# Mask rows by a POOL transfer, chunk bounds in another PSUM bank, and a planner that counts DMA transposes as late

## The chip, the cores and the metric

The kernel runs on one core of one Trainium2 chip. The metric is the device time of one execution in microseconds (us); the median of 8 runs is given with the lowest and the highest. The engines are TensorE (PE; PEld is its weight load), VectorE (DVE), ScalarE (ACT), GpSimd (POOL) and SyncE (SP). PE writes to PSUM, which has eight banks; the other working memory is SBUF. POOL and SP issue the DMA transfers here.

## What is computed

Attention in which each query sees only a few chunks of keys, followed by a feed-forward layer (FFN) with a squared relu:

```python
B, H, S, D = 4, 8, 768, 64          # chunk = 32, nc = 24, top_k = 6
k_min, k_max = min and max of k over each chunk
ub = sum over d of maximum(q * k_min, q * k_max)          # bound of each query and chunk
ub = where(causal by chunk, ub, -1e9)
top_chunks = argsort(ub)[..., -top_k:]
scores = (q @ k.T) / sqrt(D)
scores = where(chunk in top_chunks and pos_q >= pos_k, scores, -1e9)
attn = softmax(scores);  a = attn @ v
x = a as [3072 tokens, 512]
out = maximum(x @ w_in, 0) ** 2 @ w_out                   # w_in 512 x 2048, w_out 2048 x 512
```

The first 128 queries of each batch have at most four chunks before them, so all of these are chosen, and no selection is made for them.

## The kernel before

**Tiling.** There are 4 batches `b`, and in each 4 head pairs `hp`, which makes 16 pairs `p = 4 b + hp`. A sequence is six tiles of 128 tokens. The first tile of every batch is handled apart (`first_attention`, and one FFN over the four first tiles); the other five tiles of a batch (NS = 5) go through two stages for each pair and then through that batch's FFN.

**Stage A of a pair** (`stage_a`) prepares the operands of its scores. Keys and queries are needed with the head dimension on the partitions. For batches 0 and 1 PE transposes them (`kT`, `qT`, in PSUM); for batches 2 and 3 (`b >= BY_DMA`) SP issues DMA transposes (L377) from loaded tiles `nt` into `kt` and `qt`. From these VectorE takes the maximum and the minimum of each chunk (`kr`, L681), and the positive and the negative part of the queries (`qp`, `qm`, L697). Ten small products on PE give the bounds `ub` (L647, L649). VectorE adds the chunk mask (`ubm`, L706), takes the eight largest (`m8`, L655) and compares (`selb`, L711). The selection is transposed to `sT` (by PE, or for batches 2 and 3 by a DMA transpose) and copied under the queries, into rows 64 to 87 of `qsc`. Rows 64 to 87 of the keys' operand `kqc` hold the mask's rows: -32768 where the chunk of that row is. So one product of 88 rows (L766) gives scores with the mask added.

**The mask's rows** (`kq_rows`, L326 to L337) are the same for all pairs. `kqc` has four sets of two heads, eight slots, which the pairs use in turn. The first slot is written by ScalarE (L328), the second is copied by a transfer that SP issues (L333), and the other six by one more transfer of SP (L335). Scores of pair 0 need the first two, those of every other pair the third step (the list `prepared` in `stage_a`).

**Stage B** (`stage_b`) runs, for each head, five score banks of 512 columns (L766), the exp on ScalarE (L788), a causal mask on the diagonal tiles by VectorE (L743) or POOL (L746), and the products with the values (L777). The sums are normalised by VectorE (L594, L596) into `x`.

**The FFN** (`ffn`) transposes `x` to `xT`, forms the hidden products `ph` (L850), takes the relu on ScalarE (L857) or VectorE (L859), squares on VectorE (`h`, L868), and adds up `py` (L881) in four parts for each 128 tokens. `py` is copied out (L271 or L273) and stored by SP (L894).

**PSUM banks.** Each buffer has a tag, and a tag a number of banks: `tp` 1, `ps` 3, `av` 2, `ff` 2. Scores, the bounds `ub` and PE's `sT` all have the tag `ps`; `kT` and `qT` have `tp`; `ph`, `py` and PE's `xt` have `ff` (in the last batch `ph` has `ps`). A buffer is given a bank when the last reader of an earlier buffer of its tag is done.

**What sets the order.** Nothing is scheduled by hand. Every operation is recorded with a cost on each engine that may run it, a due time, the operations that it needs and its buffers (`Plan.op`). `Plan.order` then plays the program: it looks for the operation that can start first, takes among those of that engine within a small wait the one that is due first, and books its cost. `Transfers` plays the two DMA queues, one for POOL's loads and one for what SP issues, which share a rate. The sequence found is written out, and each engine runs its part in that order. The due times hang on the parameters `P`: `lead` says how many steps of the plan ahead of its turn each pair's stage A is due, `f_due` the same for the first tiles, `rate` and `due` spread the FFNs, `va`, `vm`, `ra` and `h2` shift single kinds, and `loads` and `later` are the order of POOL's loads. Only POOL's loads have a fixed order; each also waits until no more than eight are on their way. In `loads`, a small letter with a number is that head pair of batch 0 (two transfers), a capital is the first tile of that batch, and `i` and `o` are quarters of the two weight matrices.

Of the kernel before, what the change touches and what calls it, by code (L numbers as in the profile page):

```python
# [9 lines left out]
F32 = mybir.dt.float32  # L10
# [31 lines left out]
class Transfers:  # L42
# [10 lines left out]
    def run(self, queues, until):  # L53
        now = self.now
        while now < until and any(queues.values()):
            active = [q for q in queues.values() if q]
            rate = self.RATE / len(active)
            span = min([until - now] + [q[0][1] / rate for q in active])
            now += span
            for q in active:  # L60
                q[0][1] -= span * rate
                if q[0][1] < 1e-6:
                    op = q.pop(0)[0]
                    op.end = now + (0.85 if op.turns else 0.35)
        return until if until < 1e8 else now
# [12 lines left out]
class Plan:  # L78
# [19 lines left out]

    def op(self, where, due, fn, needs=(), tiles=(), packets=0, turns=False):
        op = Op(where, due, fn, [n for n in needs if n is not None],  # L100
                [t for t in tiles if t is not None], packets, turns)
        for t in op.tiles:
            t.users.append(op)
        op.number = -1 if packets and not turns else len(self.ops) - len(self.loads)
        self.ops.append(op)
        if packets and not turns:
            self.loads.append(op)
        return op
# [92 lines left out]
def kernel(  # L201
# [9 lines left out]
    nc = tc.nc  # L211
# [19 lines left out]
    NSET = 4  # L231
    P = dict(lead=[38, 70, 77, 66, 65, 20, 16, 23, 34, 24, 32, 68, 19, 63, 66, 67],
             f_due=[-89, -30, -320.97, -400.97], sp='K0 Q0 K1 Q1', rows=-379,
             rows_after=0, up_due=-1.28, up_rate=3.88, half=4, due=[-6, 1, 3, 45],
             rate=[3.07, 2.84, 4.48, 1.87], va=13.9, vm=5.92, ra=2.68, h2=-1.11,
             later='k1 q1 v1 q2 k2 q3 v3 v2 k3', shift={}, p0=-5650, wait=0.01,
             loads="k0 Q3 K3 q0 Q2 K2 V0 V3 V2 V1 v1 "
                   "k1 i0 v0 i3 q1 i2 v2 k2 i1 q2 o0 q3 k3 o1 o2 v3 o3")

# [86 lines left out]
    def kq_rows(i):  # L326
# [5 lines left out]
        elif i == 1:  # L332
            nc.sync.dma_start(out=kqs[D:KC, 0, 1], in_=kqs[D:KC, 0, 0])  # L333
        else:
            nc.sync.dma_start(  # L335
                out=kqs[D:KC, 1:].rearrange("c s hh j -> c (s hh) j"),
                in_=kqs[D:KC, 0, 0:1].to_broadcast([NC, 2 * NSET - 2, S]))  # L337
# [11 lines left out]
    def load(key, fn, due, packets, tiles=(), cost=0.88):  # L349
        op = plan.op({"POOL": cost}, due, fn, tiles=tiles, packets=packets)  # L350
        loaded.setdefault(key, []).append(op)
# [23 lines left out]

    def turn_by_dma(dst, src, due, needs, tiles, packets=1270):
        return plan.op({"SP": 1.2}, due, lambda _: nc.sync.dma_start_transpose(  # L377
            out=dst(), in_=src()), needs, tiles, packets=packets, turns=True)

# [35 lines left out]
    def load_turned(nm, b, j, due):  # L415
# [3 lines left out]
        else:  # L419
# [9 lines left out]
            lambda: (src.tile if src else firsts[nm][:, b]).rearrange(  # L429
                "p h d -> p (h d)"), due, needs, [src, dst])  # L430
        loaded.setdefault((nm, b), []).append(op)
# [46 lines left out]
    for what in P["loads"].split():  # L478
        i = int(what[1])
        if what[0] == "i":  # L480
            load_w_in(4 * i, 4 * i + 4, -980)
        elif what[0] == "o":
            load_w_out(4 * i, 4 * i + 4, -980)
        elif what[0].isupper():
            load_first(what[0].lower(), i, -980)
        else:
            load_pair(what[0], 0, i, -980)
# [113 lines left out]
    def rows(after):  # L601
        made["rows", 0] = plan.op({"ACT": 0.84}, P["rows"], lambda _: kq_rows(0),
                                  [made["ident"]] + after)
        for i in (1, 2):
            made["rows", i] = plan.op({"SP": 0.5}, P["rows"] + i, lambda _, i=i: kq_rows(i),
                                      [made["rows", 0]], packets=(200, 1200)[i - 1],
                                      turns=True)

# [4 lines left out]
    def stage_a(p):  # L613
# [10 lines left out]
        qp, qm = buffer("qp", [128, QC]), buffer("qm", [128, QC])  # L624
        ub = buffer("ps", [128, NS, 2, NC], F32, name="ub")
        ubm = buffer("ubm", [128, NS, 2, NC], F32)
# [42 lines left out]
        if b >= BY_DMA:  # L669
            got = list(loaded["k", b])  # L670
            kc_on, qc_on, q_on = {"DVE": 0.36}, {"DVE": 0.40}, 0.39
        else:
# [42 lines left out]
        if b >= BY_DMA:  # L715
            t = turn_by_dma(lambda: sT.tile, lambda: selbs[:, s].rearrange(
                "p t h c -> p (t h c)"), t0 + 21, [sel], [sT], 950)
        else:
# [88 lines left out]
    def ffn(x, ready, rows, by_dma, due, rate, up_tags=("ff", "ff")):  # L807
# [12 lines left out]
        def turn(t):  # L820
            if by_dma:
                xt_made.append(turn_by_dma(
                    lambda: xT[:, t], lambda: x[:, t], step(0.225), ready(t),
                    [xT] + xs))
                return
# [14 lines left out]
        def up(f, c0, c1, i):  # L840
            tag = up_tags[i % 2]
            w = c1 - c0
# [78 lines left out]
    for b in range(B):  # L921
        x = buffer("x", [128, NS, d_model])
        x_done[b, 1] = []
        for p in range(NP * b, NP * (b + 1)):
# [4 lines left out]
            x, lambda t, b=b: x_done[b, 1], [S * b + 128 * t for t in range(1, NT)],  # L929
            0 < b < B - 1, HALVES * NP * (b + 1) + P["due"][b], P["rate"][b], ("ps", "ps") if last else ("ff", "ff"))  # L930
        for c in range(2):
# [45 lines left out]
```

## Time and profile before

| | |
|---|---|
| median of 8 runs | 265.15 us (264.58 to 266.77) |
| the profiled execution | 264.91 us, of which the span from the first to the last instruction is 263.2 us |
| mean granted clock of PE | 0.992 |
| DMA | 26.11 MB in 103808 packets, the queue of POOL's loads 66.9% of 16 engines' span |

The costliest groups, as the page gives them (line, engine, operation, tiles and shapes, count, then busy us and mean ns of one, then the idle time before them and what ended it):

```profile
L788 ACT ACTIVATE e<-ps 128x512 bf16<-128x512 f32 x160 | 89.0, 607 | 12.4 <-PE av L777 6.7
L850 PE MATMUL ph<-xT,w_in_sb 128*128 128x256 bf16 (+2 forms) x592 | 97.1, 304 | 0.4
L881 PE MATMUL py<-w_out_sb,h 128*128 128x512 bf16 (+2 forms) x400 | 92.5, 370 | 0.0
L868 DVE TENSOR_TENSOR h<-ht 128x256 bf16<-128x256 bf16 (+2 forms) x148 | 47.1, 326 | 14.4 <-ACT ht L857 10.3
L766 PE MATMUL ps<-qsc,kqc 88*128 88x128 bf16 (+1 forms) x320 | 54.7, 272 | 2.2 <-DVE ubm L706 1.5
```

A matmul's mean is longer than the time from one to the next, since they are pipelined: four products of 512 columns follow each other in 0.86 us. The span falls into a start of some 24 us, in which few tiles have landed, a long middle in which attention and FFN are interleaved, and from 206 us on only the last FFN.

### The profile page before, as it was taken

How to read it: one execution, taken by the hardware profiler on the slowest of the kernel's cores; microseconds unless marked ns; L12 is line 12 of the kernel's file. 1: busy time of each engine (PE TensorE's matmuls, PEld its weight loads, DVE VectorE, ACT ScalarE, POOL GpSimd, SP SyncE). 2: the span in 40 equal slices, each digit the busy share in tenths (PEclk: the TensorE clock that was granted, in tenths of full speed). 3: DMA queues.
4: the chain of work that ended last, by engine and by line, in shares of the span. 5: the costliest groups of instructions: out<-in, count | busy, mean ns of one | idle time of the engine just before them, and what ended most of it. 6: DMA issues, size and time to landing. Idle time of an engine off the chain costs nothing.

```text
span 263.2 us, 6518 instructions
## 1 busy us (share of the span) xinstructions
PE 252.4 (96%) x2391; PEld 162.2 (62%) x2391; DVE 195.2 (74%) x687; ACT 181.4 (69%) x372; POOL 104.9 (40%) x182
## 2 busy tenths in 40 slices
PE   7679999999999999998999999999999999999995
PEld 3447656665787665565686665567876548565443
DVE  5699899979998999999999979856777403455000
ACT  1679687974599978795888867688998315276112
POOL 8998778698347698632221221120012000000000
PEclk9799999999999999999999999999999999999999
DMA  9999999999999999964540001345000021100222
GB/s 143 167 174 186 188 181 197 157 116 196 188 99 135 143 155 155 159 115 112 114 104 4 0 2 55 87 110 115 2 0 2 0 80 42 41 4 0 80 80 80
DMA packets 103808, 26.11 MB, mean 99 GB/s; under 512 B 96312, under 2 KB 100832, under 8 KB 103776
## 3 DMA queue, kind: packets, MB, share of 16 engines
q0 software_dynamic: 75088, 13.11, 66.9%
q1 hardware_dynamic: 28688, 12.59, 21.0%
q8 instruction: 18, 0.29, 0.5%
q14 instruction: 14, 0.11, 0.1%
HBM read 27.26 MB, written 6.29 MB: 127 GB/s over the span
## 4 chain that ended last, share of the span: by engine, by line
PE 62%; DVE 17%; DMA 8%; ACT 4%; SPq 3%; issue 3%; POOL 2%; POOLq 0%; DVEq 0%; ACTq 0%
PE py L881 24%; PE ph L850 22%; PE ps L766 7%; DVE kr L681 5%; PE av L777 5%; SPq L377 3%; DMA k<-in_k_dram 2%; DMA kt<-nt 2%; DVE qsc L273 2%; DVE m L655 2%; DMA qt<-nt 2%; DVE kqc L273 2%; DMA nt<-in_q_dram 2%; ACT e L788 2%; ACT ht L857 1%
## 5 line engine op out<-in xcount | busy, mean ns | idle before, releaser
L788 ACT ACTIVATE e<-ps 128x512 bf16<-128x512 f32 x160 | 89.0, 607 | 12.4 <-PE av L777 6.7
L850 PE MATMUL ph<-xT,w_in_sb 128*128 128x256 bf16 (+2 forms) x592 | 97.1, 304 | 0.4
L881 PE MATMUL py<-w_out_sb,h 128*128 128x512 bf16 (+2 forms) x400 | 92.5, 370 | 0.0
L850 PEld LDWEIGHTS <-w_in_sb 128*128 128x128 bf16 x592 | 55.7, 97 | 23.3 <-issue 1.4
L746 POOL TENSOR_SCALAR_AFFINE_SELECT e<-e 128x128 bf16<-128x128 bf16 (+1 forms) x88 | 30.2, 345 | 93.4 <-ACT e L788 90.1
L857 ACT ACTIVATE ht<-ph 128x256 bf16<-128x256 f32 (+2 forms) x121 | 54.4, 453 | 17.6 <-PE ph L850 14.0
L868 DVE TENSOR_TENSOR h<-ht 128x256 bf16<-128x256 bf16 (+2 forms) x148 | 47.1, 326 | 14.4 <-ACT ht L857 10.3
L766 PE MATMUL ps<-qsc,kqc 88*128 88x128 bf16 (+1 forms) x320 | 54.7, 272 | 2.2 <-DVE ubm L706 1.5
L881 PEld LDWEIGHTS <-h 128*128 128x128 bf16 x400 | 35.6, 98 | 31.3
L777 PEld LDWEIGHTS <-e 128*128 128x128 bf16 x640 | 35.1, 97 | 11.8 <-DVE e L743 0.3
L271 ACT COPY ob<-py 128x512 f32<-128x512 f32 (+2 forms) x23 | 13.0, 567 | 35.0 <-PE py L881 34.9
L777 PE MATMUL av<-vn,e 128*128 128x65 bf16 x480 | 35.6, 193 | 0.0
L766 PEld LDWEIGHTS <-kqc 88*128 88x128 bf16 x320 | 26.0, 97 | 12.9 <-issue 3.7
L271 ACT COPY qsc<-sT 24x384 bf16<-24x384 bf16 (+1 forms) x39 | 17.1, 437 | 4.5 <-PE sT L276 2.5
L596 DVE TENSOR_TENSOR x<-av,rc 128x320 bf16<-128x320 f32 (+1 forms) x40 | 18.9, 471 | 0.5
L655 DVE MAX8 m<-ubm 128x8 f32<-128x24 f32 x160 | 15.5, 168 | 0.2
L681 DVE TENSOR_REDUCE kr<-kT 128x24 bf16<-128x768 bf16 x16 | 14.8, 949 | 0.4 <-PE kT L276 0.3
L681 DVE TENSOR_REDUCE kr<-kt 128x24 bf16<-128x768 bf16 x16 | 15.0, 939 | 0.0
L743 DVE TENSOR_TENSOR e<-e,tri 128x128 bf16<-128x128 bf16 (+1 forms) x40 | 9.7, 247 | 6.7 <-ACT e L788 5.9
L777 PE MATMUL av<-v,e 128*128 128x65 bf16 x160 | 14.6, 193 | 0.0
L859 DVE TENSOR_SCALAR ht<-ph 128x256 bf16<-128x256 f32 (+2 forms) x27 | 12.9, 482 | 2.2 <-PE ph L850 1.9
L273 DVE COPY xT<-xt 128x512 bf16<-128x512 bf16 x10 | 4.1, 420 | 12.3 <-PE xt L276 12.3
(85 smaller groups left out, 247.3 us busy)
## 6 DMA issues: line engine op xcount, KB each, us to landing
out_dram<-ob SPq DMA_DIRECT2D x23, 256.0 KB, 2.4
w_in_sb<-in_moe_w_in_dram POOLq DMA_DIRECT2D x4, 512.0 KB, 7.9
w_out_sb<-in_moe_w_out_dram POOLq DMA_DIRECT2D x4, 512.0 KB, 8.2
vn<-in_v_dram POOLq DMA_DIRECT2D x15, 128.0 KB, 6.3
nt<-in_q_dram POOLq DMA_DIRECT2D x10, 128.0 KB, 5.0
nt<-in_k_dram POOLq DMA_DIRECT2D x10, 128.0 KB, 5.1
kn<-in_k_dram POOLq DMA_DIRECT2D x8, 80.0 KB, 6.3
qn<-in_q_dram POOLq DMA_DIRECT2D x8, 80.0 KB, 7.6
```

The lines of the kernel that those rows point to most:

```text
L271: nc.scalar.copy(dst, src)
L596: return plan.op({"DVE": 0.06 + 0.00108 * D * n}, due, lambda _: nc.vector.tensor_mul(x(), av[:, :, 0:D], rc[:, 0:n].unsqueeze(2).to_broad ...
L655: nc.vector.max(out=m8[:, i, hh], in_=ubm[:, i, hh])
L681: nc.vector.tensor_reduce(kr[:, mm].rearrange("d (t c) -> d t c", c=128 // CH) if b >= BY_DMA else kr[:, mm], part(kT).rearrange("d t (c j ...
L746: nc.gpsimd.affine_select(out=e, in_=e, compare_op=ALU.is_ge, fill=0.0, base=0, channel_multiplier=-1, pattern=[[0, n], [1, 128]])
L766: nc.tensor.matmul(ps[:, 128 * c:128 * (c + nt)], lhsT=kqs[:, s, hh, 128 * j:128 * (j + 1)], rhs=qss[:, s, hh, 128 * (t0 - 1):128 * (t0 - ...
L777: nc.tensor.matmul(av[:, t - 1], lhsT=e[:, 128 * c:128 * (c + 1)], rhs=value_tile(b, h, j), start=(i == 0 and c == 0), stop=(i == len(BANK ...
L788: nc.scalar.activation(e.tile, ps.tile, ACT.Exp, scale=scale), [sc], [ps, e])
L850: nc.tensor.matmul(ph.tile, lhsT=w_in_sb[:, ki, 128 * f:128 * (f + 1)], rhs=xT[:, c0 // 128:c1 // 128, ki], start=(ki == 0), stop=(ki == N ...
L857: nc.scalar.activation(ht.tile, ph.tile, ACT.Relu)
L868: {"DVE": 0.067 + w / 1920}, at[0] + P["h2"], lambda _: nc.vector.tensor_mul(h2[f][:, c0:c1], ht.tile, ht.tile), [op], [ht, h2[f]])))
L881: nc.tensor.matmul(py.tile, lhsT=h2[f][:, 128 * t:128 * (t + 1)], rhs=w_out_sb[:, f, c0:c1], start=(f == 0), stop=(f == NFI - 1))
```

## The change

Four things are changed in the program, and all parameters of the plan with them.

1. The third step of the mask's rows (six slots of `kqc`) is issued by POOL instead of SP, as one of its loads: it stands as `R2` in `loads`, behind the third head pair of keys. It still waits for the first slot.
2. The bounds `ub` of pairs 8 to 15 have the tag `tp` instead of `ps`.
3. The plan adds a time `late` to the end of DMA transfers: 0.5 for loads, 4.5 for the transposes of keys and queries, 3.5 for those of selections, 3.0 for those of `x`. It is a number in the planner alone.
4. The costs that the plan books on VectorE for copies of DMA-transposed tiles go from 0.36, 0.40 and 0.39 to 0.45, 0.45 and 0.42, and the transfer of the second slot is booked with 400 packets instead of 200.

```diff
-                    op.end = now + (0.85 if op.turns else 0.35)
+                    op.end = now + (0.85 if op.turns else 0.35) + op.late
...
-    P = dict(lead=[38, 70, 77, 66, 65, 20, 16, 23, 34, 24, 32, 68, 19, 63, 66, 67],
-             f_due=[-89, -30, -320.97, -400.97], sp='K0 Q0 K1 Q1', rows=-379,
-             rows_after=0, up_due=-1.28, up_rate=3.88, half=4, due=[-6, 1, 3, 45],
-             rate=[3.07, 2.84, 4.48, 1.87], va=13.9, vm=5.92, ra=2.68, h2=-1.11,
-             later='k1 q1 v1 q2 k2 q3 v3 v2 k3', shift={}, p0=-5650, wait=0.01,
-             loads="k0 Q3 K3 q0 Q2 K2 V0 V3 V2 V1 v1 "
-                   "k1 i0 v0 i3 q1 i2 v2 k2 i1 q2 o0 q3 k3 o1 o2 v3 o3")
+    P = dict(lead=[26, 15, 48, 47, 26, 61, 5, 53, 70, 14, 26, 79, 70, 28, 8, 54],
+             f_due=[207, -206, -290.97, -438.97], sp='K0 Q0 K1 Q1', rows=-1719,
+             rows_after=0, up_due=-34.03, up_rate=11.93, half=4,
+             due=[-21, -128, -27, -2], rate=[4.44, 7.05, 5.27, 4.28], va=11.75,
+             vm=13.01, ra=0.57, h2=-0.91, later='k1 q1 v1 k2 q2 q3 v2 k3 v3', shift={},
+             p0=-7210, wait=0.01,
+             loads="k0 q0 V2 Q3 V1 K3 K2 V0 Q2 k1 V3 "
+                   "i0 q1 v0 i3 i2 v1 k2 R2 q2 i1 o0 q3 k3 o1 v2 v3 o2 o3")
...
-            nc.sync.dma_start(
+            nc.gpsimd.dma_start(
                 out=kqs[D:KC, 1:].rearrange("c s hh j -> c (s hh) j"),
                 in_=kqs[D:KC, 0, 0:1].to_broadcast([NC, 2 * NSET - 2, S]))
...
+        elif what[0] == "R":
+            load("rows", lambda _: kq_rows(2), -980, 2300)
+            made["rows", 2] = loaded["rows"][0]
...
-        for i in (1, 2):
-            made["rows", i] = plan.op({"SP": 0.5}, P["rows"] + i, lambda _, i=i: kq_rows(i),
-                                      [made["rows", 0]], packets=(200, 1200)[i - 1],
-                                      turns=True)
+        made["rows", 1] = plan.op({"SP": 0.5}, P["rows"] + 1, lambda _: kq_rows(1),
+                                  [made["rows", 0]], packets=400, turns=True)
+        made["rows", 2].needs.append(made["rows", 0])
...
-        ub = buffer("ps", [128, NS, 2, NC], F32, name="ub")
+        ub = buffer("tp" if b >= BY_DMA else "ps", [128, NS, 2, NC], F32, name="ub")
...
-            kc_on, qc_on, q_on = {"DVE": 0.36}, {"DVE": 0.40}, 0.39
+            kc_on, qc_on, q_on = {"DVE": 0.45}, {"DVE": 0.45}, 0.42
```

The remaining lines of the diff pass `late` to the transposes and replace `i % 2` by `i % len(up_tags)`, which is the same here. In both programs the same products, reductions and copies are made, but for some more products with the constant tile `warm`, which the planner puts where it expects PE to idle at the start.

## The prediction

> **What bounds the kernel now.** I read the page from the top, then the busy time by stretches, the list of waits of each engine, and last the timeline around the longest waits of TensorE.
>
> ```profile
> span 263.2 us, 6518 instructions
> PE 252.4 (96%) x2391; PEld 162.2 (62%) x2391; DVE 195.2 (74%) x687; ACT 181.4 (69%) x372; POOL 104.9 (40%) x182
> ```
>
> TensorE is busy for 252.4 of 263.2 us, so 10.8 us is all that better cover could win. The stretches say where these lie (the columns are the stretch, its length, then PE, PEld, DVE, ACT and POOL busy):
>
> ```profile
> 0.00:24.00 24.00, 18.48 (x176) 10.50 (x177) 17.82 (x71) 14.70 (x28) 22.80 (x34) 0.93 1.73 166
> 24.00:55.00 31.00, 30.64 (x329) 19.91 (x327) 29.75 (x109) 24.87 (x49) 23.52 (x37) 1.00 1.69 177
> 55.00:75.00 20.00, 19.93 (x200) 13.45 (x199) 17.46 (x57) 12.71 (x27) 12.39 (x17) 1.00 1.73 163
> 75.00:100.00 25.00, 24.88 (x271) 17.93 (x270) 23.95 (x85) 22.64 (x49) 19.21 (x29) 1.00 1.91 137
> 100.00:130.00 30.00, 28.49 (x311) 17.37 (x310) 29.50 (x103) 23.40 (x46) 13.01 (x29) 1.00 1.22 132
> 130.00:160.00 30.00, 29.72 (x280) 20.55 (x278) 28.09 (x101) 24.68 (x55) 6.92 (x19) 1.00 0.13 30
> 160.00:206.00 46.00, 46.00 (x499) 31.52 (x497) 33.85 (x126) 38.05 (x79) 7.05 (x21) 1.00 0.20 53
> ```
>
> Of the 10.8 us, 5.5 lie before 24 us (24.00 less 18.48), about 2.9 are the last copy and its store, and only 2.3 lie between 24 and 206 us. Of those, 1.5 are in one stretch, 100 to 130 us, where VectorE is busy for 29.50 of 30.00: there TensorE waits, and the engine it waits for has no room. The waits name it:
>
> ```profile
> PE ps L766 <- DVE ubm L706: 1.5, 3, 0.7
> ...
> POOL nt L421 <- issue: 1.1, 4, 0.5
> ```
>
> Scores (L766) wait three times for the add that masks the chunk bounds (L706). No operand passes between these two: `ub` and the scores' `ps` share one tag with three PSUM banks, and a bank is free only when the add has read it. The timeline at the first of them:
>
> ```profile
> 103.25 0.60 PE L766 MATMUL ps<-qsc,kqc 88*128 88x128 bf16 x4
> 103.68 0.53 PE L777 MATMUL av<-vn,e 128*128 128x65 bf16 x12
> 104.05 0.22 PE L777 MATMUL av<-v,e 128*128 128x65 bf16 x2
> 104.11 0.23 PE L777 MATMUL av<-vn,e 128*128 128x65 bf16 x2
> 104.88 0.60 PE L766 MATMUL ps<-qsc,kqc 88*128 88x128 bf16 x4 [0.55 <-DVE ubm L706]
> ```
>
> The bounds were written at 103.0 to 103.2; the add ran only at 104.42, behind two reductions of 0.94 each.
>
> **The change, part by part.** The diff turns nearly every knob of the planner, so the order of all engines is new; I compared the two orders of instructions (they hold no time) and priced what differs by rows of this trace. Where I count TensorE work between two instructions, 512 columns cost 0.216 us (the chain has four such products in 0.86), a value product 0.03, a bounds product 0.027.
>
> *Bounds of pairs 8 to 15 into the transposes' bank.* `tp` has one bank, used by the transposes of pairs 0 to 7 alone and so empty afterwards. All three named waits, at 104.88, 120.47 and 129.48, come from such bounds (0.55 + 0.66 + 0.28 = 1.5). In the new order the users of `tp` from pair 8 on stand at least 3.9 us of TensorE work apart, and scores are never behind these adds. Start to start the first wait is nearer 0.7 (104.88 less the last value product at 104.14), so at most about -2.0; if VectorE's lag only shows up at the next consumer, 0. I take **-1.5**. What hides the late add now: the selection made from it goes into scores some ten microseconds of TensorE work later (pairs 8 to 12).
>
> *Scores' banks.* Without these bounds the reuse loosens: counted in the orders, scores that start less than 1.0 us of TensorE work after the previous scores of their bank go from six to three. The exp that empties a bank takes 0.607 in the mean row, and with hand-overs at both ends a gap of 0.64 to 0.89 is short by about 0.2 each: 3 x 0.2, **-0.6**, bounds -1.0 and 0.
>
> *Rows for seven mask copies by a POOL transfer.* It leaves SP at 11.13 us (0.85 of SP, which then waits till 57.60, so nothing there gains) and stands behind the third pair of key loads. While it ran, loads that had landed 0.8 to 1.3 apart came 2.4 apart (15.33, 17.70), later catching up: about 1.1 us of transfer time leaves the start. Behind the reordered loads, the first slice of the input weights should land near 20.7 instead of 22.82 (two value loads of 0.5 each and these 1.1 fewer ahead of it). But the first hidden product at 23.84 has other things ahead of it as well, so 0 (bounds -1.1 and +0.6). The new place: POOL pays one issue more, by its load rows 0.9 us, with free time of 2 us between 26 and 31 us; queued behind it are loads of pairs needed after 40 us. It should land at about 31.5, and its first reader, the scores of pair 1, stands some 23 us of TensorE work in, about 36 us on the clock: 4.5 us of cover. If that cover is gone, pair 1 waits microsecond for microsecond.
>
> Here a rule speaks against the change. The rows: POOL's loads took 0.855 to 1.1 us each while VectorE was busy for 29.75 of 31.00 (24 to 55 us), so descriptors were never held up by more than a fifth of a microsecond. The Trainium skill ("SBUF — State Buffer", section "A bandwidth-pool intuition that's wrong (but worth ruling out)") says that a transfer issued by GpSimd can be starved while VectorE holds the port that they share, 620 ns becoming 3100. By that rule the copy would come up to 2.5 us later, still inside its cover; by the row, not at all.
>
> *The start.* Query tiles of pair 0 load third instead of fifth, so VectorE's wait of 0.73 before `qp` at 13.58 goes, and ScalarE takes two query copies (0.69 against 0.49). But the preset and value products of batch 1 stand ahead of the bounds on TensorE, and batch 1's exps come after those copies. Walked by rows, bounds are at 14.45 (14.56 before), the selection ends 0.2 earlier, ScalarE's first exp of pair 0 is at 22.1 instead of 20.36, and the first hidden product at about 22.9, against 23.84, with 0.9 us less TensorE work ahead of it, so level. By the ninth hidden block I get half a microsecond late. Value **+0.3**, bounds -0.7 and +1.2.
>
> *Late transposes and truer copy costs.* These alter only the plan. SP's transposes take 1.2 each and land 1.2 to 4.6 after issue; POOL's next loads wait for their buffers (the 1.1 above, off the path). They come later now, behind more selects, and q2's last lands near 93 us with its reader at about 104. 0, bounds -0.5 and +0.5.
>
> *Where the new order is tighter.* In the FFN of batch 0 the first output tile is opened while the last hidden blocks still run, holding one of the two `ff` banks: eight hidden blocks of 384 columns then share the other, with 0.7 to 1.5 us of TensorE work between them. Emptying takes 0.495 on ScalarE plus about 0.3 of hand-over when ScalarE is free. Two of eight short by 0.1: **+0.2**, bounds 0 and +3.2. Pair 13's selection transposes now stand on SP behind four of x (1.25 each), and land about 1 us ahead of need: **+0.1**, bounds 0 and +1.0.
>
> *Sum:* -1.5 - 0.6 + 0.3 + 0.2 + 0.1 = -1.5. The profiled run took 264.91 with its span of 263.2 (1.7 around it), so it becomes 263.4; the median of the eight runs shown is 0.24 above it: **263.7**.
>
> **The rivals.** *One bank for eight hidden blocks* (slower). Place: L850 between the first and last part of batch 0's first output tile, some 84 to 97 us. ScalarE was busy for 22.64 of 25.00 there, so a relu may stand behind an exp of 0.6. Price 0.4 each, 8 x 0.4 = 3.2 instead of the 0.2: 266.7. It decides once emptying takes over 1.0 us. For it: that busy share, and truly one bank. Against: VectorE can take relus too, and in this trace relus waited 14.0 us for products, not the reverse.
>
> *VectorE is the bound anyway* (no change). The waits for the adds go, but 29.50 of 30.00 stays, and copies of selections on VectorE grow from 25 to 35 (0.29 each, 3 us, spread out), so TensorE meets late masks and squares instead: the -1.5 and -0.6 return, the tighter places remain in part: 265.2. Against it: up to the bounds of pair 11, VectorE's work ahead of need is about 0.7 more than before, but it had 4.1 us idle between 55 and 130.
>
> *Rows late* (slower): starvation plus queueing eat 4.5 us and one more: 264.7 to 266; I give it little.
>
> **How the numbers follow.** Forecast as summed, with its bounds 261.4 to 264.3: 0.54. No change 0.15. One bank 0.27, rows late 0.04. Leaving out about one in ten on each side gives 261.4 to 267.2. A measurement of this kernel tells about 0.3% (0.8 us) from no change: faster 0.54, same 0.16, slower 0.30.
>
> **What would show it.** Right: no wait of scores for L706 after 100 us; TensorE idle between 100 and 130 us under 0.5; first hidden product at 22.5 to 23.5; rows landed by 33 us; hidden blocks at 84 to 97 us without idle over 0.3. Wrong: TensorE waiting for VectorE's masks or squares in 100 to 130 us, hidden products spaced by relus near 90 us, or a start later than 24 us.

## The result, and the profile after

The kernel after is a little slower: 266.63 us median (266.11 to 267.2, 11 runs) against 265.32 (264.15 to 267.13, 32 runs) of the kernel before on the same chip; the ratio is 1.0048, 95% interval 1.0029 to 1.0067, so 0.8 to 1.8 us. The prediction had the sign wrong. The profiled execution took 266.27 us with a span of 264.6.

The head of the page, and the stretches (the stretch, its length, then PE, PEld, DVE, ACT and POOL busy):

```profile
span 264.6 us, 6553 instructions
PE 254.1 (96%) x2403; PEld 163.7 (62%) x2403; DVE 197.8 (75%) x699; ACT 180.0 (68%) x366; POOL 102.9 (39%) x177
```

```profile
55.00:75.00 20.00, 19.48 (x193) 12.53 (x192) 16.98 (x54) 12.64 (x26) 11.84 (x15) 1.00 2.19 181
75.00:100.00 25.00, 24.70 (x276) 17.75 (x276) 24.01 (x80) 23.81 (x51) 13.12 (x30) 1.00 1.02 96
100.00:130.00 30.00, 29.92 (x307) 18.43 (x306) 29.24 (x111) 21.21 (x43) 19.39 (x31) 1.00 1.65 137
```

What the change was expected to win is won: between 100 and 130 us TensorE idles 0.08 us instead of 1.51. It is given back elsewhere: 0.5 of idle time between 55 and 75 us, where there was 0.07, and 0.3 between 75 and 100, where there was 0.12. The waits of TensorE name the new place:

```profile
PE ph L857 <- ACT ht L864: 1.2, 5, 0.3
...
PE ph L857 <- DVE ht L866: 0.6, 1, 0.6
```

No wait of scores for the masking add is left (1.5 before). At the top stand hidden products (L857, L850 before) that wait for a relu. As with the bounds, no operand passes between them: a hidden block may only start when the relu of an earlier block has emptied its PSUM bank. TensorE and then ScalarE at the worst place (start, duration, engine, line, operation, in brackets the idle time before it):

```profile
71.99 0.60 PE L857 MATMUL ph<-xT,w_in_sb 128*128 128x256 bf16 x4 [0.18 <-ACT ht L864]
72.49 0.34 PE L279 MATMUL sT<-ident,selb 128*128 128x128 bf16 x3
73.11 1.03 PE L857 MATMUL ph<-xT,w_in_sb 128*128 128x256 bf16 x8 [0.28 <-ACT ht L864]
...
75.25 1.03 PE L857 MATMUL ph<-xT,w_in_sb 128*128 128x256 bf16 x8 [0.30 <-ACT ht L864]
```

```profile
71.96 0.69 ACT L274 COPY qsc<-qT 64x640 bf16<-64x640 bf16 x1
72.67 0.38 ACT L864 ACTIVATE ht<-ph 128x256 bf16<-128x256 f32 x1
73.08 1.71 ACT L274 COPY qsc<-sT 24x384 bf16<-24x384 bf16 x4
74.81 0.38 ACT L864 ACTIVATE ht<-ph 128x256 bf16<-128x256 f32 x1
```

The block at 75.25 follows the relu at 74.81, which stood behind four copies of selections; the product that this relu empties had ended at about 74.0. The brackets understate the loss, since a matmul's listed duration reaches past the start of the next: from one start to the next, less the time of the columns, these three places cost 0.35, 0.45 and 0.46.

The three are not alike. At 71.99 and 73.11 the order itself is tight: between the two uses of the bank lie only 0.43 and 0.16 us of TensorE work, and a relu takes 0.38. At 75.25 there are 0.75 us between them, and it is the relu that comes late. The longest loss, 0.74 from start to start, is of this second kind. The products in its bank had ended at 35.1 us, and VectorE came to their relu only at 38.39:

```profile
38.39 1.28 DVE L866 TENSOR_SCALAR ht<-ph 128x512 bf16<-128x512 f32 x2
```

```profile
39.12 1.89 PE L857 MATMUL ph<-xT,w_in_sb 128*128 128x512 bf16 x8 [0.58 <-DVE ht L866]
```

Two tables follow, worked out from the traces in that way. The first gives the time at which each kernel had done the same TensorE work (without the products with `warm`):

| kernel before, us | 34 | 45 | 66 | 77 | 87 | 98 | 109 | 119 | 131 | 142 | 152 | 182 | 203 | 254 |
|---|---|---|---|---|---|---|---|---|---|---|---|---|---|---|
| kernel after, later by | 0.1 | 0.7 | 0.2 | 1.1 | 1.6 | 1.8 | 1.1 | 1.0 | 0.4 | -0.3 | 0.7 | 0.6 | 1.3 | 1.2 |

So the new order loses 1.6 us between 66 and 98 us, wins 2.1 from there to 142, and loses 1.5 more behind that. The second sorts the TensorE time lost from 34 us on by what ended each gap:

| TensorE time lost, us | before | after |
|---|---|---|
| hidden products waiting for a relu | 1.6 | 3.9 |
| scores waiting for the masking add | 2.0 | 0 |
| all else | 6.3 | 7.2 |
| sum | 9.9 | 11.1 |

How short a gap still counts as a wait moves the split: with other limits the first row grows by 2.1 to 2.8 us instead of 2.3, and "all else" by less or more.

### The profile page after: what moved, and what is told of

Its sections match the earlier page's. It is cut to its first block, busy times and chain, and to the rows that moved or that the text cites. A ratio compares the mean times of both kernels' runs of the same rounds, so it can differ in the third digit from the quotient of the medians.

```text
span 264.6 us, 6553 instructions
## 1 busy us (share of the span) xinstructions
PE 254.1 (96%) x2403; PEld 163.7 (62%) x2403; DVE 197.8 (75%) x699; ACT 180.0 (68%) x366; POOL 102.9 (39%) x177
## 4 chain that ended last, share of the span: by engine, by line
PE 76%; DVE 11%; ACT 5%; POOL 3%; DMA 2%; issue 2%; POOLq 0%; ACTq 0%; DVEq 0%
PE py L888 28%; PE ph L857 25%; PE ps L773 10%; PE av L784 6%; DMA kn<-in_k_dram 2%; DVE h L875 2%; ACT qsc L274 2%; POOL vn L439 2%; DVE kr L688 1%; ACT ht L864 1%; DVE qsc L276 1%; DVE m L662 1%; DVE kqc L276 1%; PE xt L279 1%; PE T L279 1%
## 5 line engine op out<-in xcount | busy, mean ns | idle before, releaser
L857 PE MATMUL ph<-xT,w_in_sb 128*128 128x256 bf16 (+2 forms) x592 | 96.4, 304 | 2.1 <-ACT ht L864 1.2
L795 ACT ACTIVATE e<-ps 128x512 bf16<-128x512 f32 x160 | 87.0, 608 | 9.7 <-PE ps L773 7.4
L857 PEld LDWEIGHTS <-w_in_sb 128*128 128x128 bf16 x592 | 56.2, 97 | 27.1 <-issue 4.5
L864 ACT ACTIVATE ht<-ph 128x384 bf16<-128x384 f32 (+2 forms) x120 | 53.6, 452 | 19.5 <-PE ph L857 15.9
L753 POOL TENSOR_SCALAR_AFFINE_SELECT e<-e 128x128 bf16<-128x128 bf16 (+1 forms) x82 | 27.8, 342 | 92.9 <-ACT e L795 83.9
L875 DVE TENSOR_TENSOR h<-ht 128x256 bf16<-128x256 bf16 (+2 forms) x148 | 46.8, 330 | 19.9 <-ACT ht L864 13.1
L773 PE MATMUL ps<-qsc,kqc 88*128 88x128 bf16 (+1 forms) x320 | 53.2, 272 | 0.0
L784 PEld LDWEIGHTS <-e 128*128 128x128 bf16 x640 | 33.5, 97 | 10.4 <-POOL e L753 0.5
L784 PE MATMUL av<-vn,e 128*128 128x65 bf16 x480 | 34.2, 193 | 0.1
L750 DVE TENSOR_TENSOR e<-e,tri 128x128 bf16<-128x128 bf16 (+1 forms) x46 | 10.3, 232 | 8.1 <-ACT e L795 7.5
L439 POOL DMA_DIRECT2D vn<-in_v_dram x15 | 13.2, 889 | 0.6 <-issue 0.4
L274 ACT COPY qsc<-sT 24x256 bf16<-24x256 bf16 (+1 forms) x29 | 12.5, 432 | 1.1 <-PE sT L279 0.5
```

Source lines behind the costliest of these rows:

```text
L274: nc.scalar.copy(dst, src)
L439: load((nm, b), lambda _: nc.gpsimd.dma_start(out=nat[nm, b].tile[:, j - 1, :, 0:D], in_=SRC[nm][b, :, 128 * j:128 * (j + 1)].rearrange("h ...
L753: nc.gpsimd.affine_select(out=e, in_=e, compare_op=ALU.is_ge, fill=0.0, base=0, channel_multiplier=-1, pattern=[[0, n], [1, 128]])
L773: nc.tensor.matmul(ps[:, 128 * c:128 * (c + nt)], lhsT=kqs[:, s, hh, 128 * j:128 * (j + 1)], rhs=qss[:, s, hh, 128 * (t0 - 1):128 * (t0 - ...
L784: nc.tensor.matmul(av[:, t - 1], lhsT=e[:, 128 * c:128 * (c + 1)], rhs=value_tile(b, h, j), start=(i == 0 and c == 0), stop=(i == len(BANK ...
L795: nc.scalar.activation(e.tile, ps.tile, ACT.Exp, scale=scale), [sc], [ps, e])
```

## The experiments

Each kernel was timed in five rounds beside the kernel before on the same chip. The medians of the kernel before lay between 265.3 and 266.5 us from one series, and chip, to the next, so ratios to it are compared: the kernel after is at 1.0048. "Order kept" means that every engine executes the same operations in the same order as in the kernel named, and only a tile's PSUM bank or an instruction's engine is another: the planner still sees the old tag. The first 14 us of single executions differ by up to 1.6 us, with the landing of the first loads; where two traces are compared step by step, this difference is taken off.

### The parts alone, in the old order

Bounds of pairs 8 to 15 in the transposes' bank (`b_tp`), the third rows copy on POOL (`b_rows`), and both (`b_both`):

```diff
-        ub = buffer("ps", [128, NS, 2, NC], F32, name="ub")
+        ub = buffer("ps", [128, NS, 2, NC], F32, name="ub",
+                    place="tp" if b >= BY_DMA else "ps")
...
-            nc.sync.dma_start(
+            nc.gpsimd.dma_start(
...
+    plan.moves = [(made["rows", 2], loaded["k", 0, 2][1])]
```

> The kernel before with its order of instructions kept on every engine; only the bounds of pairs 8 to 15 are written into the transposes' bank instead of a scores' bank (the planner still counts them with the scores). Theory A (this part gains what the prediction said, and the loss lies in the re-tuned order): the waits of scores for the masking add, 1.5 us, go, and some of the tight scores' banks too; -1.5 to -2, so 263.3 to 263.8 us beside 265.3, TensorE idle under 0.5 between 100 and 130 us. Rival B (VectorE is the bound there): the waits come back as waits for masks, squares or selections; 265.0 to 265.5, idle near 1.5.

> The kernel before with its order kept; only the copy of the mask rows of the later pairs is issued by POOL, right after the third pair of later key loads, instead of by SP at 11 us. Theory A (hidden either way): 264.8 to 265.4 us; rows landed by 33 us; the first slice of input weights lands up to 1.1 us earlier, and the first hidden product not more than 0.5 earlier. Rival B (the rows are late, or POOL's later loads are): scores of pair 1 wait for them; 266 to 267.

> The kernel before with its order kept and both parts in it: bounds of pairs 8 to 15 in the transposes' bank and the third rows copy on POOL. Theory A (both parts are harmless by themselves, the order is what costs): 262.8 to 263.8 us, 3 us less than the kernel after. Rival B (the parts cost it): no faster than the kernel before, 265 or more.

Measured: `b_tp` 265.87 us, ratio 0.9991 (0.9969 to 1.0013); `b_rows` 265.92, 0.9999 (0.9969 to 1.0028); `b_both` 266.25, 1.0010 (0.9982 to 1.0037). The rows cost nothing on either engine, as theory A had it. The bank is worth nothing either in the old order, where 1.5 to 2 us were expected. The waits of TensorE in `b_tp` between 100 and 135 us show where they went (the profiled execution is the longest of its twelve, 267.74 us):

```profile
PE ph L856 <- DMA xT<-x: 1.6, 1, 1.6
PE ps L772 <- DVE ubm L712: 0.5, 1, 0.5
PE ub L653 <- DVE ubm L712: 0.4, 1, 0.4
```

Three different things. The wait of 0.5 is the first of the old three, at 105 us, and it stayed: the bounds behind it are those of pair 7, the last pair of batch 1, which are not moved. The second went from scores to the next bounds: in the old order two pairs' bounds stand 0.27 us of TensorE work apart, and there is only one transposes' bank. The third was followed at once by a wait for transposes of `x`, which landed at 130.9 us; in the kernel before they had landed at 129.2, under the wait for the add. `b_both` has the same wait, 1.5 us long. Why they land later with the bounds moved is not shown.

### The parts undone, in the new order

Bounds back in the scores' banks (`a_ps`), and the third rows copy back on SP (`a_rows_sp`):

```diff
-        ub = buffer("tp" if b >= BY_DMA else "ps", [128, NS, 2, NC], F32, name="ub")
+        ub = buffer("tp" if b >= BY_DMA else "ps", [128, NS, 2, NC], F32, name="ub",
+                    place="ps")
```

```diff
-            nc.gpsimd.dma_start(
+            nc.sync.dma_start(
...
+    plan.moves = [(made["rows", 2], made["rows", 1])]
```

> The kernel after with its order kept; only the bounds of pairs 8 to 15 go back into the scores' banks. Theory A (the bank gains about 2 us in the new order, which other waits outweigh): 267.6 to 268.6 us, waits of scores for the masking add come back. Rival B (the bank is worth nothing, as VectorE sets the pace): 266.4 to 266.9. Rival C (the bank itself costs something): under 266.3.

> The kernel after with its order kept; only the third rows copy goes back to SP, right behind the second. Theory A (who copies the rows does not matter): 266.3 to 267.0 us. Rival B (the POOL copy and its place cost something): under 266.2, with scores of pair 1 or POOL's loads earlier. Rival C (the copy on SP holds up the first loads, as thought in the prediction): over 267.0, and first input weights about 1 us later.

Measured: `a_ps` 269.78 us, ratio 1.0145 (1.0117 to 1.0174); `a_rows_sp` 267.16, 1.0045 (1.0027 to 1.0064). The rows are worth nothing here too. The bank is worth 1.0145 - 1.0048 = 0.97%, 2.6 us (give or take 0.9, by the two intervals), more than the 1 to 2 us that theory A had. The waits between 100 and 206 us in `a_ps` that the kernel after doesn't have:

```profile
PE ub L660 <- ACT e L801: 1.1, 3, 0.6
PE ps L779 <- ACT e L801: 0.8, 2, 0.5
PE ps L779 <- DVE ubm L719: 0.5, 1, 0.5
```

Most of them are not the scores' wait for the add: bounds wait for an exp to empty a scores' bank, and scores for exps. The same edit is worth nothing in one order and 2.6 us in the other. So what outweighs it must lie in the order, and the rest of the experiments is about that.

### Banks for the hidden blocks that wait

`a_av` puts four hidden blocks of batch 0 into the attention's two banks while these are idle; `a_banks` does so at all the places of the new waits (the diff is that of `a_banks`; `a_av` has only the first of the four entries).

```diff
-            ph = buffer(tag, [128, w], F32, name="ph")
+            ph = buffer(tag, [128, w], F32, name="ph",
+                        place=spare.get((f, c0)))
...
+    SPARE = [{(f, 0): "av" for f in (3, 4, 6, 8)}, {(7, 256): "tp", (9, 256): "av"},
+             {(6, 0): "tp", (10, 0): "tp"}, {}]
...
-                         P["up_due"], P["up_rate"])
+                         P["up_due"], P["up_rate"], spare={(2, 0): "av", (11, 0): "av"})
```

> The kernel after with its order kept; only four hidden blocks of batch 0 (numbers 3, 4, 6 and 8, on TensorE at 71 to 76 us) are written into the attention's two banks, idle from 65 to 78 us, instead of the two of the FFN. Theory A (these blocks wait for banks that the relus empty): the waits at 71.99, 73.11 and 75.25 us, 1.26 start to start, go; 265.2 to 265.8 us beside 266.6. Rival B (the relus' engines are behind anyway, so the wait moves to the products' readers or to later blocks): 266.3 to 266.8.

> The kernel after with its order kept; ten hidden blocks that waited for a bank, or whose bank the waiting one needed, go into banks idle at that time: two of the first FFN's (23.1 and 39.1 us) and the four of the run before into the attention's, two of batch 1 at 144.8 and 146.8 us and two of batch 2 at 183.8 and 186.5 us into the transposes' or the attention's. Theory A (the relus' banks are what the new order costs): the waits, 0.69 + 0.74 + 1.26 + 0.64 + 0.39 = 3.7 start to start, go for the most part; 262.8 to 264.3 us, less than the kernel before. Rival B (ScalarE and VectorE are the bound, banks only show it): not under 265.5.

Measured: `a_av` 266.69 us, ratio 1.0032 (1.0013 to 1.0051); `a_banks` 266.58, 1.0020 (0.9999 to 1.0041). Both point down, by 0.4 and 0.7 us, but the intervals overlap that of the kernel after, and neither is near the 1.3 and 3.7 that the waits add up to. Step by step, the trace of `a_av` is 0.45 earlier against the kernel after at 73 us, 0.65 at 75, and only 0.28 from 81 us on. All three waits are gone, 1.26 from start to start, and 0.94 comes back behind them, each time as a wait for VectorE: 0.34 for a selection where the second of these lines shows it, in TensorE's timeline of `a_av`, 0.25 between two bounds at 75.2 to 75.4 us (for `qm`), 0.23 for the next selection and 0.12 for a relu.

```profile
72.39 1.47 PE L863 MATMUL ph<-xT,w_in_sb 128*128 128x256 bf16 x12
74.11 0.34 PE L284 MATMUL sT<-ident,selb 128*128 128x128 bf16 x3 [0.24 <-DVE selb L723]
```

Three hidden blocks now run without a gap, and the transpose behind them waits for a selection of VectorE instead. In `a_banks` waits that the kernel after doesn't have come up behind the ones removed at 145 to 148 us and at 184 to 187:

```profile
150.08 0.81 PE L863 MATMUL ph<-xT,w_in_sb 128*128 128x384 bf16 x4 [0.56 <-DVE ht L872]
```

```profile
189.59 1.03 PE L863 MATMUL ph<-xT,w_in_sb 128*128 128x256 bf16 x8 [0.44 <-DVE ht L872]
```

From start to start, 0.78 is won at the first place and 0.72 lost at 150 us; 0.39 is won at the second and 0.57 lost at 189.6. The 0.74 won at 39 us is lost again by 45, all of it to VectorE, whose relu of the next block takes 0.48. What stays of the 3.7 is 0.57 at 23 to 25 us and the 0.28 of `a_av`, less the 0.2 at 190 us: 0.6 in all, which agrees with the 0.7 of the medians.

### Less work for VectorE at that place

`a_av_nosq` is `a_av` without ten squares: the relu of these blocks writes the slice of `h` itself, so they are not squared.

```diff
+            plain = spare and c0 == 0 and f < 10
+            if plain:
+                ht.make = straight
...
-                {"DVE": 0.067 + w / 1920}, at[0] + P["h2"], lambda _: nc.vector.tensor_mul(
+                {"DVE": 0.067 + w / 1920}, at[0] + P["h2"], lambda _: None if plain else nc.vector.tensor_mul(
```

> The kernel with four hidden blocks of batch 0 in the attention's banks, and besides the squares of the first ten hidden blocks of batch 0 left out (VectorE, 69 to 76 us; the relu writes what the square would have written, so the output differs): 10 x 0.25 = 2.5 us less of VectorE there, everything else in place. Theory A (with the banks given, VectorE's selections are what TensorE waits for at 72 to 76 us): another 0.6 to 1.0 us less than with the banks alone, 265.6 to 266.1, and no wait for selections there. Rival B (VectorE is not what holds it): 266.4 to 266.8.

Measured: 266.82 us, ratio 1.0024 (1.0003 to 1.0046). Beside `a_av` that is no difference that can be told, and from 81 us on its trace is 0.59 earlier than the kernel after, where `a_av` is 0.28. So the selections were not the limit for long: the wait of 0.24 for one is down to 0.10, but taking 2.5 us from VectorE gave only 0.3, and the next selection's transpose, at 77.1 us, waits 0.16 (0.32 from start to start) for an exp of ScalarE. The time is that of rival B. By the trace VectorE did hold a part: what comes back as waits for it falls from 0.94 to 0.39, and 0.39 comes back as waits for ScalarE instead.

### Other engines for some copies and relus

`a_split` gives nine instructions to the other engine; `a_mix` adds the spare banks.

```diff
+        if p == 1:
+            for c in cs[0] + cs[1]:
+                c.on = "ACT"
+        if p == 9:
+            for c in (cs[0] + cs[1])[:3]:
+                c.on = "DVE"
...
+            if n == B and f in (11, 14):
+                op.on = "ACT"
```

> The kernel after with its order kept; only nine instructions change engine: the four selection copies of pair 1 (VectorE, 32.6 to 33.9 us) and the relus of two hidden blocks of the first FFN (VectorE, 38.4 and 39.0 us) go to ScalarE, which idles 4 us between 30 and 38 us; three selection copies that stand between relus on ScalarE (143.75, 144.80, 145.73 us) go to VectorE. Theory A (in the new order copies and relus stand on the wrong one of two full engines, and TensorE waits for that): the waits at 37.08, 39.12, 144.82 and 146.81 us, 0.45 + 0.74 + 0.64 = 1.8 start to start, go; 264.8 to 265.6 us. Rival B (VectorE and ScalarE together are full, whoever does what): 266.2 to 266.9, as waits move.

> The run before with the spare banks as well: one block of the first FFN and four of batch 0 in the attention's banks, four of batches 1 and 2 in the transposes' or the attention's. Theory A: 264.0 to 265.0 us, less than the kernel before. Rival B: 266.0 or more.

Measured: `a_split` 268.43 us, ratio 1.0098 (1.0081 to 1.0115); `a_mix` 267.9, 1.0078 (1.0061 to 1.0096). Both are slower than the kernel after; `a_split` is slower than either theory had, `a_mix` is in rival B's range. ScalarE in `a_split`:

```profile
35.81 0.60 ACT L875 ACTIVATE ht<-ph 128x512 bf16<-128x512 f32 x1
36.73 1.57 ACT L806 ACTIVATE e<-ps 128x512 bf16<-128x512 f32 x3 [0.32 <-PE ps L784]
38.31 1.39 ACT L279 COPY qsc<-qT 64x640 bf16<-64x640 bf16 x2
39.72 0.60 ACT L875 ACTIVATE ht<-ph 128x512 bf16<-128x512 f32 x1
```

```profile
40.37 2.00 PE L868 MATMUL ph<-xT,w_in_sb 128*128 128x512 bf16 x8 [1.07 <-ACT ht L875]
```

The idle time of ScalarE at 30 to 38 us lay before its exps, and the relu handed to it came behind them: it ran at 39.72 (39.1 without the later start of this execution), after VectorE's time for it (38.4), and TensorE waited 1.07 instead of 0.58. The other moves lost too: ScalarE's new copies at 33.45 hold up a relu (0.6 us of TensorE from start to start), and the three copies given to VectorE come late for scores at 147 us (0.4) and delay a relu of its own (0.8 at 152). Idle time on an engine in order is of use only if it lies where the plan's sequence has the instruction.

### The old order with the moved bounds' waits taken away

`b_best` tries to keep the gain of the bank in the old order: pair 7's bounds in the transposes' bank as well, pair 9's not, and one selection's transpose behind the transposes of `x`.

```diff
+                    place="tp" if p >= 7 and p != 9 else "ps")
...
+    plan.moves = [(made["sT", 11], made["turned", 1][1])]
```

> The kernel before with its order kept on every engine but SP: the bounds of pairs 7, 8, 10 and 11 to 15 in the transposes' bank, those of pair 9 left in the scores' (they follow pair 11's within 0.3 us of work), and the selection transpose of pair 11 on SP behind the first two transposes of x instead of ahead. Theory A (in the old order the bank was worth nothing because the first wait was pair 7's, the second moved to the next bounds, and the third to late transposes of x): the waits at 104.88, 120.47 and 129.48 us go and the transposes of x land in time; 264.0 to 264.8 us beside 265.7. Rival B (another wait for VectorE takes their place): 265.3 or more.

In the old order pair 9 is prepared after pair 11. Measured: 266.62 us, ratio 1.0053 (1.0026 to 1.0079). By 121 us the trace is 1.5 earlier than the kernel before: the first two waits are gone. At 129.45 us it is 0.85 later, for

```profile
128.48 1.45 ACT L276 COPY qsc<-sT 24x384 bf16<-24x384 bf16 x3 [3.23 <-DMA sT<-selb]
```

```profile
129.45 0.81 PE L773 MATMUL ps<-qsc,kqc 88*128 88x256 bf16 x6 [1.78 <-ACT qsc L276]
```

The selection that was put back on SP is needed at 128 us already: ScalarE waits 3.23 us for it, and the scores 1.78 for ScalarE.

### A plan made anew with the old numbers

`a_oldP` is the kernel after with the old due times, rates and loads (`R2` behind `k2`).

```diff
-    P = dict(lead=[26, 15, 48, ...
+    P = dict(lead=[38, 70, 77, ...
...
+                   "k1 i0 v0 i3 q1 i2 v2 k2 R2 i1 q2 o0 q3 k3 o1 o2 v3 o3")
```

> The kernel after with the due times, rates and load order of the kernel before (the rows copy placed after the third pair of later key loads): the three parts with a plan made anew, without the re-tuned numbers. Theory A (the parts gain, the re-tuned numbers lose): 263.3 to 265.0 us. Rival B (a plan made for the truer costs and lateness is worse by itself): over 266.0, with TensorE waiting for relus or masks.

Measured: 273.92 us, ratio 1.0297 (1.0262 to 1.0331), with scores waiting 2.4 for exps and 2.3 for a copy. So the numbers of the plan cannot be taken apart from its costs and banks. This run does not tell whether the truer costs are bad by themselves, only that a plan with numbers not chosen for it loses some 8 us.

### Two orders joined

The last five kernels have every engine follow one kernel's order up to a point and the other's from there, read from a list of operations.

```diff
-        for op in self.order():
+        for op in self.listed:
...
+    for word, engine in zip(ORDER.split(), ENGINES):
+        k, _, fill = word.partition("+")
+        op = named[k]
...
+        plan.listed.append(op)
```

> Two orders joined: every engine follows the order of the kernel before up to about 100 us and the order of the kernel after from there on (same operations, same code, bounds of pairs 8 to 15 in the transposes' bank). At equal TensorE work the profiled kernel after is 1.8 us behind the kernel before at that point and 1.2 behind at the end. Theory A (what the new order costs is made between 67 and 100 us, where its hidden blocks wait, and what it gains comes after): 0.5 to 0.6 less than the kernel before, ratio 0.998. Rival B (the element engines are equally full in either order, and what the first part saves comes back as waits in the second): no less than the kernel before, ratio 1.002 or more.

> Three pieces: the order of the kernel before to about 100 us, of the kernel after from there to about 150 us (the bounds' bank at work), of the kernel before again to the end. Theory A: another 0.5 less than with two pieces, as the new order's waits at 184 to 187 us go: 1.1 us less than the kernel before, ratio 0.996. Rival B: as the kernel before or slower, ratio 1.000 or more.

> The order of the kernel after to about 170 us, of the kernel before from there on. Theory A (the last 0.5 us of the loss lies in the hidden blocks of batch 2 at 184 to 187 us): 0.5 less than the kernel after, ratio to the kernel before 1.003. Rival B: as the kernel after, ratio 1.005.

> The order of the kernel before to about 67 us, where both orders have done the same work on TensorE and ScalarE, and the order of the kernel after from there on (bounds of pairs 8 to 15 in the transposes' bank). By the profiles the kernel after is 0.2 us behind at that point and 1.2 at the end. Theory A (the loss is made after 67 us by the new order): ratio to the kernel before 1.004 (+1.0 us). Rival B (it is made before 67 us, by loads, rows and first FFN): ratio 1.001 or less.

> The other way round: the order of the kernel after to about 67 us, of the kernel before from there on (bounds of pairs 8 to 15 in the transposes' bank, which in the old order was worth nothing). Theory A: ratio to the kernel before 1.000 to 1.001 (+0.2 us). Rival B: 1.004 or more.

Measured, as ratios: `h_100` 1.0228 (1.0193 to 1.0263), `h_100_150` 1.0435 (1.0396 to 1.0475), `h_170` 1.0303 (1.0259 to 1.0348), `h_old_new_67` 1.0821 (1.0778 to 1.0865), `h_new_old_67` 1.0118 (1.0062 to 1.0174). As totals they tell nothing, for the joint itself costs more than what was to be told apart: at 100, 150 and 170 us the orders differ by 1 to 3 us of work on VectorE and ScalarE, and at 67 us, where TensorE and ScalarE have done nearly the same, still in the loads that POOL has issued; behind a load that waits, POOL's masks wait too. From the list of POOL's waits of `h_old_new_67` between 60 and 110 us, then from the lists of TensorE's waits, of `h_old_new_67` and of `h_new_old_67`:

```profile
POOL nt L575 <- DMA kt<-nt: 26.4, 4, 8.4
```

```profile
PE av L933 <- POOL e L902: 20.2, 1, 20.2
...
PE ph L1006 <- ACT ht L1013: 1.0, 4, 0.3
```

```profile
PE qT L428 <- DVE kr L837: 1.2, 1, 1.2
...
PE ph L1006 <- DVE ht L1015: 0.6, 1, 0.6
```

What they do tell is in the last line of each of TensorE's lists. The kernel after has five waits for ScalarE's relus and one of 0.6 for VectorE's. The new order up to 67 us with the old one behind it has the one of 0.6, one of ScalarE's (0.2, between 20 and 30 us, so in its new part as well) and none of the other four; the old order to 67 us with the new one behind it has four of ScalarE's, though all of it runs 20 us late. So these waits belong to the new order of their own stretch, whatever went before. Lost TensorE time by stretches says the same: the stretch that is 182 to 209 us in the kernel before loses about 0.7 there, in `h_170` and in `h_new_old_67`, and about 1.3 in the kernel after, in `h_100` and in `h_old_new_67`.

No version is faster than the kernel before by more than its interval; `a_banks` comes nearest of those in the new order, at 1.0020 (0.9999 to 1.0041).

## Why the prediction was wrong

The step that failed is "Where the new order is tighter", and in it the term +0.2 with its bounds 0 and +3.2. It priced one place, where a single `ff` bank serves eight hidden blocks. There the loss is what it was: three of the blocks wait 0.11 to 0.16 us from start to start, 0.4 in all, the kernel before loses 0.4 in that stretch too, and TensorE is busy for 12.96 of 13.00 us from 84 to 97 us (12.88 before). The waits of all other hidden products were put at nothing, without a reason. From 34 us on these waits went from 1.6 to 3.9 us, +2.3, above all at 39, 72 to 75, 145 to 147 and 184 to 187 us. With the 2.0 won at the adds and 0.9 in small waits the sum is +1.2, which is what the traces show at the end.

Two things make them. At 73 us the banks are reused too soon: the uses are 0.16 and 0.43 us of work apart in the new order, and nowhere closer than 0.59 in the old one at that place. The counting done for the scores' banks would have found this. At the other places the uses are 0.75 to 2.8 us apart, while in the old order uses 0.76 apart lose nothing at 95 to 97 us. There the relu is late, because its engine has other work queued ahead: copies of selections on ScalarE before 75.25, 144.8 and 146.8, and reductions, squares, copies and `MAX8` on VectorE before 39.1, 183.8 and 186.5. The prediction's time for emptying a bank held "when ScalarE is free", and at these places neither engine was.

The other steps:

- *Bounds into the transposes' bank, -1.5.* Mechanism right, size 0.5 short: the waits for the add are gone, 2.0 from start to start. The working was wrong in one point: "All three named waits ... come from such bounds". The first was pair 7's, which `b_tp` left in place; it vanished in the kernel after because the order there is another.
- *Scores' banks, -0.6.* Not borne out. The close uses do go from six to three, but waits for exps at them cost TensorE only 0.2 in the kernel before (at 49.6 and 52.1 us) and cost 0.2 in the kernel after (at 114.9 and 122.8). The 2.6 that the bank is worth by `a_ps` is no proof of this step: there it is mostly bounds that wait for exps, and scores in other places.
- *Rows by a POOL transfer, 0.* Right, by two runs; it fills six slots, not seven. POOL issued it at 24.3 us in 0.675 and it landed 8.4 later, at 32.7, where 31.5 was estimated and landing by 33 was the sign. The Trainium skill ("SBUF — State Buffer", section "A bandwidth-pool intuition that's wrong (but worth ruling out)") gives its 3100 ns for a transfer beside a VectorE `tensor_copy`. Its rule was not put to the test by this transfer: VectorE was busy for 30.11 of 31.00 us between 24 and 55 us, but while POOL issued the copy of the rows (24.27 to 24.95) it ran products of two tensors alone (L875, L750). The rows that the prediction set against the rule, 0.855 to 1.1, differ by a quarter of a microsecond, not a fifth.
- *The start, +0.3.* The first hidden product came at 21.8 us, earlier than the 22.5 to 23.5 given, though its weights landed at 21.4 and not 20.7. At 34 us, with the same work done, the kernel after is 0.1 late. The size was off by 0.2.
- *Late transposes and truer copy costs, 0.* Not settled: `a_oldP` mixes them with numbers that don't fit. From issue to landing the transposes take 2.3 to 7.0 us in the kernel before, not 1.2 to 4.6. *Pair 13's transposes, +0.1:* no wait for them shows.

Of the five signs for "right" four came true, and none of those for "wrong": they watched the start, 84 to 97 and 100 to 130 us, and the loss lay elsewhere. Of the rivals, "One bank for eight hidden blocks" named the right kind of wait, a hidden product that a relu holds up. That its time came so near (266.7 against 266.6) is luck: its place lost no more than before, and its 3.2 were eight blocks at 0.4 there. "VectorE is the bound anyway" fails for the kernel after at 100 to 130 us, where no idle time is left, but is much of what the old order shows: there `b_tp` wins 0.8 and 0.4 and `b_best` 1.5 us, and waits for VectorE's next result, a transpose or ScalarE take it back within 10 us. In the new order too, what comes back from 39 us on in `a_av` and `a_banks` is waits for VectorE.

Shown is that the waits of hidden products belong to the new order of their stretches, that taking three of them away gives back about a fifth (0.28 of 1.26 in `a_av`, by the traces), and all of them together 0.6 of 3.7. Shown too is what takes the rest back, place by place: VectorE, and where VectorE had less to do, ScalarE. That VectorE, ScalarE and the banks are all within 0.2 to 0.5 us of being late there is a reading of these, not a measurement of its own. So where the time is lost is known, and why the planner's new order as a whole cannot be freed of it stays open. How much that order would give without the hidden blocks' gaps stays open as well, since the joined orders were spoiled by their joints.

## What to carry to other kernels

When a planner's order changes as a whole, count for every PSUM tag, not only for the one that the change is about, how much work of the writing engine lies between two uses of a bank, and look for what the emptying engine has queued ahead. Where three engines are each busy for over 90% of a stretch (from 71 to 81 us TensorE 92%, VectorE 96%, ScalarE 98%), a wait's length is no estimate of what its removal gives: from 39 us on it gave here between a fifth and nothing. And a part that is worth nothing in one order can be worth 2.6 us in another, so a part should be tried in the order in which it is to run.

## What the runs showed of the hardware

DMA transposes landed later where loads shared the time. Between 118 and 137 us, in the kernel before, with no load of POOL there (median from issue to landing last), and then in the kernel after, with six:

```profile
xT<-x SPq DMA_TRANSPOSE x5, 2.5
kt<-nt SPq DMA_TRANSPOSE x3, 2.5
```

```profile
vn<-in_v_dram POOLq DMA_DIRECT2D x5, 128.0 KB, 7.6
nt<-in_k_dram POOLq DMA_DIRECT2D x1, 128.0 KB, 4.2
xT<-x SPq DMA_TRANSPOSE x5, 5.2
kt<-nt SPq DMA_TRANSPOSE x5, 5.9
```

These are two orders, with 11 and 13 transposes in the stretch, and not one order with the loads taken away. Without any load near them their landing still differs: in `b_tp` those of `x` took 2.5 to 4.9 us from issue (4.7 in `b_both`), in the kernel before 2.5 to 3.2, and the later landing cost 1.6 us there.

A hidden product that waits for its bank starts some 0.05 us after the end of the relu: the relu that starts at 74.81 and takes 0.38 ends at 75.20, and the product starts at 75.25.
